# Attention scores in tiles of 64 queries of two heads, and the first row list ahead of the expert weights

## The chip, the cores and the metric

One core of one Trainium2 chip runs the whole program in one launch. The metric is the device time in microseconds (us); times before were taken in three runs, and one more execution was profiled.

## The reference

Three layers follow each other, all in float32 at the interface. Sliding-window attention with a linear distance penalty (4 batches, 8 heads, 576 positions of width 64):

```
scores = q @ k^T / 8 - slope[h] * |i - j|      where 0 <= i - j < 128, else -1e9
attn   = exp(scores - max) / (sum(exp) + 1e-9);   x = attn @ v      # 2304 rows x 512
```

Then a mixture of 8 experts: each row goes to the expert with the largest gate logit and gets `gate * (relu(x @ w1[e]) @ w2[e])`, w1 512x1024 and w2 1024x512. Then a bilinear layer: `((x @ w1) * (x @ w2) @ w3) @ w_out`, with its weights in float64.

## The kernel before

TensorE works on pairs of float32r numbers: every operand is split into a high and a low part, and a product is three matmuls, high by high, high by low, low by high (`mm3`, L278 to 281). A split is one ScalarE write (high) and one VectorE subtraction (low); in the first eight full chunks (`PE_LO = 9`) the low part of q and k is taken by a further matmul with a scaled identity instead (`split_pe`, L272 to 276, the matmul at L273), and ScalarE writes both parts.

**Attention.** A batch has four chunks of 128 queries and a tail of 64. A unit is half a chunk: two pairs of heads. There are 40 units: 24 full ones (chunks 1 to 3), 8 of chunk 0, whose window is 128 keys, and 8 tails. For a full unit, `scores` (L364) has 12 matmuls, each of one head: 64 rows of the array, 128 queries, 256 keys; head 0 of a pair lies in partitions 0 to 63 and head 1 in 64 to 127, and each writes its own PSUM tile S. A tail has both heads in one matmul of 128 rows: 64 queries of each side by side in the columns, with zeros between (`qz`), and 192 keys (`mm3`, so its lines are L279 to 281). `softmax` adds the bias and takes the smallest value in one VectorE instruction (L390), and ScalarE takes exp and the row sum (L395). `p_transposes` turns P on TensorE (L416) into one-bank PSUM tiles, tag P, two buffers: a full unit has eight transposes in two tiles, and two copies by ScalarE (L417). `attend` multiplies by v (L452). `gate_logits` transposes the result back beside the gate weights (L484), VectorE scales by 1/sum (L490), and the rows go to DRAM (`xz`). Row sums get 1e-9 and a reciprocal on VectorE (L462, L463); a tail's P is scaled before its transposes (L401 to 404).

**Beside it** run the folding of the bilinear layer's w3 and w_out into one matrix (transposes L721, products `pw`), conversions from float64 on VectorE (L676 to 689) and routing: `route` ranks a group of tiles, and GpSimd scatters row numbers into the list `inv2` (L556). What of the w3 products is left over comes behind attention.

**Hand-over.** `block_table` computes the first expert and row. `first_loads` lets the load queue (SyncE, SP in the profile) issue three weight loads of 512 KB (`load_w`, L932) and then the list of rows (`gather_x`: ids, L947), with which GpSimd gathers x (L953). The block's transposes (L974, `btp`) and splits follow, and the first expert matmuls write `ph`.

**Order.** The program is traced by a framework whose planner simulates the engines with a cost model and orders each engine's instructions by that; the engines then work in that order. Work beside the units has its places in lists by unit (`W_STEPS`, `LEAD`, `WO_AT`), which the change leaves alone.

Of the kernel before, what the change touches and what calls it, by code (L numbers as in the profile page):

```python
# [44 lines left out]
def kernel(  # L45
# [56 lines left out]
    a_p = astk.enter_context(tc.tile_pool(name="ap", bufs=2))  # L102

    def pst(tag, shape, name, bufs=2):
        return ps.tile(shape, F32, tag=tag, name=name, bufs=bufs)
# [10 lines left out]
    one_r = a_p.tile([P, H], F32, tag="one_r", name="one_r", bufs=1)  # L116
# [30 lines left out]
    bias = a_p.tile([P, H, 2 * P], F32, tag="bias", name="bias", bufs=1)  # L147
    bias_t = a_p.tile([P, H // 2, P + TAIL], F32, tag="bias_t", name="bias_t", bufs=1)
    qz = [
        [a_p.tile([P, H // 2, P], F32R, tag=f"qz{i}{j}", name=f"qz{i}{j}", bufs=1) for j in range(2)]  # L150
        for i in range(2)
    ]

# [16 lines left out]
    def build_constants():  # L170
        scr = a_p.tile([P, 3, 2 * P], F32, tag="p", name="scr", bufs=2)
        rel_i, rel, msk = scr[:, 0, :].bitcast(I32), scr[:, 1, :], scr[:, 2, :]
# [4 lines left out]
        )  # L177
        for t, f in ((id_k, -1.0), (id_q, 1.0 / SCALE)):
            nc.vector.tensor_scalar_mul(t, ident, f)

        nc.gpsimd.iota(rel_i, pattern=[[-1, 2 * P]], base=P, channel_multiplier=1)
        nc.gpsimd.tensor_copy(rel, rel_i)
        nc.gpsimd.memset(msk, 0.0)
        for t, fill in ((rel, 0.0), (msk, MASK)):
            nc.gpsimd.affine_select(
                out=t, in_=t, pattern=[[-1, 2 * P]], compare_op=ALU.is_ge, fill=fill,
                base=P, channel_multiplier=1,
            )
            nc.gpsimd.affine_select(
                out=t, in_=t, pattern=[[1, 2 * P]], compare_op=ALU.is_ge, fill=fill,  # L190
                base=-1, channel_multiplier=-1,
            )
        for h in range(H):
            slope = 2.0 ** (-8.0 * (h + 1) / H)
            nc.vector.scalar_tensor_tensor(
                out=bias[:, h, :], in0=rel, scalar=slope, in1=msk, op0=ALU.mult, op1=ALU.add
            )
# [8 lines left out]
        for i in range(2):  # L206
            for j in range(2):
                nc.gpsimd.memset(f32(qz[i][j]), 0.0)
# [4 lines left out]
    def build_constants2():  # L213
        hv = bias.rearrange("p (a t) w -> p a t w", t=2)
        nc.sync.dma_start(out=bias_t[TAIL:, :, :], in_=hv[:TAIL, :, 1, : P + TAIL])
        nc.gpsimd.tensor_copy(bias_t[:TAIL, :, :], hv[:TAIL, :, 0, : P + TAIL])
        nc.gpsimd.memset(wgx[:, :, P:], 0.0)
        nc.gpsimd.tensor_copy(wgx[:, :, :P], ident.unsqueeze(1).to_broadcast([P, ND, P]))
        nc.gpsimd.memset(one_r, 1.0)
# [50 lines left out]
    def split_pe(hi, lo, tp, scale=1.0):  # L270

        nc.scalar.activation(out=hi, in_=tp, func=AF.Copy, scale=scale)  # L272
        nc.tensor.matmul(  # L273
            tp, lhsT=id_q if scale != 1.0 else id_k, rhs=hi, start=False, stop=True, skip_group_check=True,
        )
        nc.scalar.activation(out=lo, in_=tp, func=AF.Copy, scale=scale)
# [27 lines left out]
    def transposes_q(b, c, hps=range(NP)):  # L304
        tp = pst("A", [P, NP, P], f"qtp_{b}_{c}_{hps[0]}")
        head_transposes("q", b, c, tp, hps)
        if c < NF:
            if (b, c) not in qT:
                qT[b, c] = tuple(
                    a_p.tile([P, NP, P], F32R, tag=f"qT{x}", name=f"qT{x}_{b}_{c}") for x in "hl"  # L310
                )
            hi, lo = qT[b, c]
            sl = slice(hps[0], hps[-1] + 1)
            sp = split_pe if pe_lo(b, c) else split
            sp(hi[:, sl, :], lo[:, sl, :], tp[:, sl, :], scale=-SCALE)
        else:
            hi, lo = qT[b, c] = qz[b % 2]
            for j in range(2):
                r = slice(j * D, (j + 1) * D)
                cs = slice(j * TAIL, (j + 1) * TAIL)  # L320
                split(hi[r, :, cs], lo[r, :, cs], tp[r, :, :TAIL], scale=-SCALE)
# [19 lines left out]
    st_V = {}  # L341

    def win(c):

        if c == 0:
            return 0, P
        if c < NF:
            return (c - 1) * P, 2 * P
        return (NF - 1) * P, P + TAIL

    def scores(b, c, hq):

        k0, nk = win(c)
        kh, kl = kT[b]
        qh, ql = qT[b, c]
        ks = slice(k0, k0 + nk)
        s = [pst("S", [P, 2, 2 * P], f"S_{b}_{c}_{hq}_{j}") for j in range(2 if c < NF else 1)]
        for t in range(2):
            hp = 2 * hq + t
            if c < NF:  # L360
                for i, (l, r) in enumerate(((qh, kh), (qh, kl), (ql, kh))):
                    for j in range(2):
                        d = slice(j * D, (j + 1) * D)
                        last["s"] = nc.tensor.matmul(  # L364
                            s[j][:, t, :nk], lhsT=l[d, hp, :], rhs=r[d, hp, ks],
                            start=(i == 0), stop=(i == 2),
                        )
            else:
                last["s"] = mm3(s[0][:, t, :nk], qh[:, hp, :], ql[:, hp, :], kh[:, hp, ks], kl[:, hp, ks], True, True)
        st_S[b, c, hq] = s  # L370

    def softmax(b, c, hq):
        k0, nk = win(c)
        s = st_S.pop((b, c, hq))
        if hq == 0:
            sums[b, c] = a_p.tile([P, H], F32, tag="sums", name=f"sums_{b}_{c}")
        sm = sums[b, c]
        p = a_p.tile([P, 2, 2, 2 * P], F32, tag="p", name=f"p_{b}_{c}_{hq}", bufs=2)
        mn = a_p.tile([P, 4], F32, tag="mn", name=f"mn_{b}_{c}_{hq}")
        for t in range(2):  # L380
            hp = 2 * hq + t
            for j in range(2 if c < NF else 1):
                if c == 0:
                    bi = bias[:, 2 * hp + j, P:]
                elif c < NF:
                    bi = bias[:, 2 * hp + j, :]
                else:
                    bi = bias_t[:, hp, :]
                m1 = mn[:, 2 * t + j : 2 * t + j + 1]
                nc.vector.tensor_tensor_reduce(  # L390
                    out=p[:, j, t, :nk], in0=s[j][:, t, :nk], in1=bi, scale=1.0, scalar=BIG,
                    op0=ALU.add, op1=ALU.min, accum_out=m1,
                )
                col = 2 * hp + j if c < NF else hp
                nc.scalar.activation(  # L395
                    out=p[:, j, t, :nk], in_=p[:, j, t, :nk], func=AF.Exp, scale=-1.0,
                    bias=m1, accum_out=sm[:, col : col + 1],
                )
        if c == NF:
            r1 = a_p.tile([P, 2], F32, tag="r1", name=f"r1_{b}_{hq}")  # L400
            nc.vector.tensor_scalar_add(r1, sm[:, 2 * hq : 2 * hq + 2], 1e-9)  # L401
            nc.vector.reciprocal(r1, r1)
            for t in range(2):
                nc.vector.tensor_scalar_mul(p[:, 0, t, :nk], p[:, 0, t, :nk], r1[:, t : t + 1])
        st_P[b, c, hq] = p

    def p_transposes(b, c, hq):
        p = st_P.pop((b, c, hq))
        pT = a_p.tile([P, 2, 2, 2, P], F32, tag="pT", name=f"pT_{b}_{c}_{hq}")
        if c < NF:  # L410
            nkb = 1 if c == 0 else 2
            for j in range(2):
                pt = pst("P", [P, 2, 2, P], f"PT_{b}_{c}_{hq}_{j}")
                for t in range(2):
                    for kb in range(nkb):
                        nc.tensor.transpose(pt[:, t, kb, :], p[:, j, t, kb * P : (kb + 1) * P], ident)  # L416
                nc.scalar.copy(pT[:, j, :, :nkb, :], pt[:, :, :nkb, :])  # L417
        else:
            pt = pst("P", [P, 2, 2, P], f"PT_{b}_{c}_{hq}")
            for t in range(2):  # L420
                nc.tensor.transpose(pt[:, t, 0, :], p[:, 0, t, :P], ident)
                nc.tensor.transpose(pt[:TAIL, t, 1, :], p[:, 0, t, P : P + TAIL], ident)
            nc.scalar.copy(pT[:, 0, :, 0, :], pt[:, :, 0, :])
            nc.vector.tensor_copy(pT[:TAIL, 0, :, 1, :], pt[:TAIL, :, 1, :])
        st_T[b, c, hq] = pT

    def attend(b, c, hq):
# [11 lines left out]
        if c < NF:  # L439
            kbs = [(0, c)] if c == 0 else [(0, c - 1), (1, c)]  # L440
        else:
            kbs = [(0, NF - 1), (1, NF)]
        for t in range(2):
            hp = 2 * hq + t
            for i_k, (kb, cc) in enumerate(kbs):
                n_k = P if cc < NF else TAIL
                for j in range(2):
                    if c < NF:
                        rhs = pT[:, j, t, kb, :]
                    else:  # L450
                        rhs = pT[:n_k, 0, t, kb, j * TAIL : (j + 1) * TAIL]
# [6 lines left out]
        if hq == NQ - 1:  # L458
            st_V.pop((b, c))
            if c < NF:  # L460
                r = a_p.tile([P, H], F32, tag="r", name=f"r_{b}_{c}", bufs=3)
                nc.vector.tensor_scalar_add(r, sums[b, c], 1e-9)  # L462
                nc.vector.reciprocal(r, r)  # L463
                r_t[i] = r
            else:
                r_t[i] = one_r
# [429 lines left out]
    astk.close()  # L896

# [45 lines left out]
    def gather_x(b):  # L943
# [3 lines left out]
        nc.sync.dma_start(  # L947
# [558 lines left out]
```

## Time and profile before

| | us |
|---|---|
| median of 3 runs (lowest to highest) | 776.46 (775.78 to 778.09) |
| profiled execution, its own time | 777.34 |
| its span, first to last instruction | 775.6 |
| busy: TensorE, VectorE, ScalarE, GpSimd | 750.5, 527.1, 349.5, 76.9 |

PE is TensorE's matmuls and PEld its weight loads; DVE is VectorE, ACT ScalarE, POOL GpSimd, SP the queue that issues most loads. Matmuls are pipelined: a row's length holds the fill of the array, so what one costs the engine is read from the starts. Attention takes until about 230 us of the span, the expert blocks begin at 266.60, and the bilinear layer follows to the end.

### The profile page before, as it was taken

Reading aid. Unit: us, or ns where it says so; the run is one execution under the profiler, and the core shown is the slowest. Engines: PE = TensorE matmul, PEld = TensorE weight load, DVE = VectorE, ACT = ScalarE, POOL = GpSimd, SP = SyncE. Lnnn points to the kernel's source line nnn. Section 1 sums busy time; section 2 is a strip of 40 time slices with the busy share of each in tenths; the row PEclk is TensorE's granted clock in tenths of the full one; section 3 lists DMA queues with packets and bytes.
Section 4 is the critical chain, followed back from the end, with each engine's and each line's share of the span. In section 5 each row is a group of like instructions: output and inputs, shape, how many; then the busy total and the mean of one; then the engine's idle time right before and its main releaser. Section 6 shows DMA issues by size and latency. Waiting matters only on the chain. (4 is left out here: it accounts for less than half of the span.)

```text
span 775.6 us, 12357 instructions
## 1 busy us (share of the span) xinstructions
PE 750.5 (97%) x4335; PEld 638.1 (82%) x4335; DVE 527.1 (68%) x1345; ACT 349.5 (45%) x778; POOL 76.9 (10%) x104
## 2 busy tenths in 40 slices
PE   7899999999998899999999999999999999999996
PEld 5777787777776688888888878999789997899974
DVE  3688896768589459697894345688656776567721
ACT  4786775766752333433343435432543225423131
POOL 5000200200111402021020000000120001200011
PEclk9999997899999999999999999999999999999999
DMA  7998465265127747969696335643116432234011
GB/s 139 327 304 224 110 177 144 68 147 154 42 65 142 240 123 229 292 198 341 189 302 189 120 103 180 207 136 123 63 45 200 127 111 75 65 109 120 1 42 41
DMA packets 126437, 116.62 MB, mean 150 GB/s; under 512 B 69612, under 2 KB 100716, under 8 KB 126365
## 3 DMA queue, kind: packets, MB, share of 16 engines
q1 hardware_dynamic: 122749, 106.07, 47.5%
q0 software_dynamic: 3616, 9.66, 3.9%
q8 instruction: 36, 0.59, 0.3%
q14 instruction: 36, 0.29, 0.1%
HBM read 87.85 MB, written 27.68 MB: 149 GB/s over the span
## 5 line engine op out<-in xcount | busy, mean ns | idle before, releaser
L262 ACT ACTIVATE wth<-wt 128x896 fp32r<-128x896 f32 x48 | 43.0, 945 | 90.2 <-PE pP L1252 90.2
L264 DVE TENSOR_TENSOR fwl<-fw,fwh 128x1024 fp32r<-128x1024 f32 x40 | 48.7, 1224 | 51.4 <-ACT fwh L262 51.0
L262 ACT ACTIVATE fwh<-fw 128x1024 fp32r<-128x1024 f32 x40 | 42.1, 1062 | 82.6 <-PE ph L280 65.0
L395 ACT ACTIVATE p<-p,mn 128x256 f32<-128x256 f32 (+2 forms) x144 | 68.1, 475 | 22.2 <-DVE mn L390 21.9
L279 PE MATMUL ph<-xbh,fwh 128*128 128x480 f32 x160 | 62.1, 390 | 1.1 <-ACT xbh L262 0.7
L280 PE MATMUL ph<-xbl,fwh 128*128 128x480 f32 x160 | 61.5, 384 | 0.0
L280 PE MATMUL py<-Whl,fwh 128*128 128x480 f32 x160 | 61.2, 382 | 0.0
L281 PE MATMUL ph<-xbh,fwl 128*128 128x480 f32 x160 | 61.2, 382 | 0.0
L281 PE MATMUL py<-Whl,fwl 128*128 128x480 f32 x160 | 58.9, 379 | 0.0
L279 PE MATMUL po<-Whl,abh 128*128 128x512 f32 x144 | 57.2, 397 | 0.6 <-ACT abh L262 0.6
L279 PE MATMUL py<-Whl,fwh 128*128 128x480 f32 x160 | 57.8, 379 | 0.0
L281 PE MATMUL po<-Whl,abl 128*128 128x512 f32 x144 | 57.2, 398 | 0.0
L280 PE MATMUL po<-Whl,abh 128*128 128x512 f32 x144 | 57.0, 395 | 0.0
L390 DVE CUSTOM_DVE_ANT_0 p<-S,bias 128x256 f32<-128x256 f32 (+1 forms) x128 | 43.8, 384 | 15.0 <-PE S L364 12.7
L264 DVE TENSOR_TENSOR wtl<-wt,wth 128x896 fp32r<-128x896 f32 x48 | 51.8, 1083 | 2.8 <-ACT wth L262 2.8
L264 DVE TENSOR_TENSOR abl<-ab,abh 128x512 fp32r<-128x512 f32 x36 | 24.7, 691 | 41.0 <-ACT abh L262 40.9
L1261 DVE TENSOR_TENSOR c<-pA,u 128x384 f32<-128x384 f32 x48 | 26.8, 558 | 34.6 <-PE pA L1252 32.4
L452 PE MATMUL av<-pT,vr 128*64 128x128 f32 (+2 forms) x576 | 48.7, 278 | 0.0
L262 ACT ACTIVATE abh<-ab 128x512 fp32r<-128x512 f32 x36 | 22.5, 630 | 58.1 <-PE po L280 40.6
L1357 POOL DMA_INDIRECT out_dram<-o,sid x18 | 21.6, 1202 | 259.5 <-ACT o L1356 259.5
L452 PEld LDWEIGHTS av<-pT,vr 128*64 128x64 f32 (+1 forms) x576 | 32.9, 138 | 11.7 <-issue 5.3
L416 PE MATMUL PT<-ident,p 128*128 128x128 f32 x224 | 41.5, 293 | 0.3
(249 smaller groups left out, 1959.3 us busy)
## 6 DMA issues: line engine op xcount, KB each, us to landing
wt<-wT SPq DMA_DIRECT2D x48, 448.0 KB
fw<-in_moe_w_dram SPq DMA_DIRECT2D x40, 512.0 KB
raw_w<-in_moe_w_dram SPq DMA_DIRECT2D x16, 512.0 KB
raw_m<-in_moe_w_dram SPq DMA_DIRECT2D x32, 256.0 KB
wT<-ms SPq DMA_DIRECT2D x16, 448.0 KB
yT<-zf SPq DMA_DIRECT2D x20, 256.0 KB
yT<-y SPq DMA_DIRECT2D x20, 240.0 KB
x<-yT SPq DMA_DIRECT2D x12, 384.0 KB
```

Source lines behind the costliest of these rows:

```text
L262: last["a"] = nc.scalar.activation(out=hi, in_=src, func=AF.Copy, scale=scale)
L264: last["v"] = nc.vector.tensor_tensor(out=lo, in0=src, in1=f32(hi), op=ALU.subtract)
L279: nc.tensor.matmul(dst, lhsT=lh, rhs=rh, start=start, stop=False)
L280: nc.tensor.matmul(dst, lhsT=lh, rhs=rl, start=False, stop=False)
L281: return nc.tensor.matmul(dst, lhsT=ll, rhs=rh, start=False, stop=stop)
L390: nc.vector.tensor_tensor_reduce(out=p[:, j, t, :nk], in0=s[j][:, t, :nk], in1=bi, scale=1.0, scalar=BIG, op0=ALU.add, op1=ALU.min, accum_ ...
L395: nc.scalar.activation(out=p[:, j, t, :nk], in_=p[:, j, t, :nk], func=AF.Exp, scale=-1.0, bias=m1, accum_out=sm[:, col : col + 1],)
L416: nc.tensor.transpose(pt[:, t, kb, :], p[:, j, t, kb * P : (kb + 1) * P], ident)
L452: nc.tensor.matmul(av[j * D : (j + 1) * D, hp, cs], lhsT=raw["v", b, cc][:n_k, 2 * hp + j, :], rhs=rhs, start=(i_k == 0), stop=(i_k == len ...
L1261: last["d"] = nc.vector.tensor_tensor(out=out, in0=in0, in1=in1, op=op)
L1357: sc = nc.gpsimd.indirect_dma_start(out=out, out_offset=bass.IndirectOffsetOnAxis(ap=sid[g][:, j, 0:1], axis=0), in_=o, in_offset=None, bo ...
```

## The change

All units take the tail's form. A full chunk's queries become two halves s of 64; a score tile holds 64 queries of both heads of a pair (`lhsT` is `qh[:, hp, s, :]`, 128 rows, block pattern with zeros) and 192 keys, from 64 s on within the window; S is [128, 2, 192]. Chunk 0 leaves out the keys before the start (64 and 128 remain). q's parts are written by two instructions each, one for each head's partitions, straight into the zeroed pattern `qz`, and where the low part is taken by a matmul there are two of them.

P of two halves is 384 columns, so three tiles of 128 are transposed for each pair, six in a unit. The middle tile holds the last keys of half 0 and the first of half 1; its halves are copied to their places in `pTz`, whose remaining blocks are zeroed once. The PSUM tile for it has two banks and one buffer, in a pool of its own (`psp`); tag P of the later stages comes from `ps2`. The tails' P is no longer scaled; their sums go to `sums_t` and into r as the others do. Masks are built with VectorE for 192 columns, `bias_t` and its load go, and 1e-9 is added by four GpSimd instructions.

`first_loads` reads the list of rows ahead of the three weight loads.

```
     def scores(b, c, hq):
...
+        S_t = [pst("S", [P, 2, W], f"S_{b}_{c}_{hq}_{s}") for s in halves_of(c)]
         for t in range(2):
             hp = 2 * hq + t
-            if c < NF:
-                for i, (l, r) in enumerate(((qh, kh), (qh, kl), (ql, kh))):
-                    for j in range(2):
-                        d = slice(j * D, (j + 1) * D)
-                        last["s"] = nc.tensor.matmul(
-                            s[j][:, t, :nk], lhsT=l[d, hp, :], rhs=r[d, hp, ks],
-                            start=(i == 0), stop=(i == 2),
-                        )
...
+            for s in halves_of(c):
+                w0 = first_key(c, s)
+                k0 = (c - 1) * P + s * HQ
+                ks = slice(k0 + w0, k0 + W)
+                last["s"] = mm3(
+                    S_t[s][:, t, w0:], qh[:, hp, s, :], ql[:, hp, s, :], kh[:, hp, ks], kl[:, hp, ks],
+                    True, True,
+                )
...
     def transposes_q
+        if not pe_lo(b, c):
+            for r, src, h, l in parts:
+                split(h, l, src, scale=-SCALE)
+            return
+        for r, src, h, l in parts:
+            nc.scalar.activation(out=h, in_=src, func=AF.Copy, scale=-SCALE)
+        for j in range(2):
+            nc.tensor.matmul(
+                tp[:, sl, :].rearrange("p h (s q) -> p (h s) q", s=2), lhsT=id_q,
+                rhs=hi[:, sl, :, j * HQ : (j + 1) * HQ].rearrange("p h s q -> p (h s) q"),
+                start=False, stop=j == 1, skip_group_check=True,
+            )
+        for r, src, h, l in parts:
+            nc.scalar.activation(out=l, in_=src, func=AF.Copy, scale=-SCALE)
...
     def p_transposes
+        pt = psp.tile([P, 2, 4, P], F32, tag="PT", name=f"PT_{b}_{c}_{hq}")
+        pT = pTz[n_pT[0] % 2]
...
+        tiles = [0, 2] if 0 < c < NF else [2] if c == 0 else [0]
+        for t in range(2):
+            for x in tiles:
+                tp(t, x)
+        for t in range(2):
+            tp(t, 1, P if 0 < c < NF else HQ)
+        if 0 < c < NF:
+            nc.scalar.copy(pT[:, :, 0:4:3, :], pt[:, :, 0:3:2, :])
+            nc.scalar.copy(pT[HQ:, :, 1, :], pt[HQ:, :, 1, :])
+        else:
+            x = tiles[0]
+            nc.scalar.copy(pT[:, :, 3 * x // 2, :], pt[:, :, x, :])
         if c < NF:
+            nc.scalar.copy(pT[:HQ, :, 2, :], pt[:HQ, :, 1, :])
         else:
+            nc.vector.tensor_copy(pT[:HQ, :, 2, :], pt[:HQ, :, 1, :])
...
     def attend
+                        rhs = pT[:, t, 2 * kb : 2 * kb + 2, js]
...
+                for h in range(2):
+                    for j in range(2):
+                        nc.gpsimd.tensor_scalar_add(
+                            r[h * HQ : (h + 1) * HQ, :, j], sm[j * HQ : (j + 1) * HQ, h, :], 1e-9
+                        )
...
     def build_constants
+        nc.vector.tensor_scalar_add(rel[HQ:], rel[HQ:], -float(HQ))
+        nc.vector.tensor_scalar(out=msk, in0=rel, scalar1=0.0, scalar2=None, op0=ALU.is_ge)
+        nc.vector.scalar_tensor_tensor(
+            out=seen, in0=rel, scalar=float(P), in1=msk, op0=ALU.is_lt, op1=ALU.mult
+        )
+        nc.vector.tensor_tensor(out=rel, in0=rel, in1=seen, op=ALU.mult)
+        nc.vector.tensor_scalar(
+            out=msk, in0=seen, scalar1=-MASK, scalar2=MASK, op0=ALU.mult, op1=ALU.add
+        )
...
     def first_loads(b0, b1):
-        for g in range(b0 * NS, min(b0 * NS + LA, b1 * NS)):
-            load_w(g)
+
         gather_x(b0)
+        with tc.issue_after(last["ids"].ins):
+            for g in range(b0 * NS, min(b0 * NS + LA, b1 * NS)):
+                load_w(g)
```

## Rows read from the trace of the kernel before

**Rows 1.** Busy us (instructions) by stretch; then granted clock, DMA share, GB/s.

```profile
20.00:100.00 80.00, 77.93 (x604) 59.32 (x605) 63.79 (x246) 60.84 (x188) 4.18 (x4) 0.98 0.86 243
100.00:225.00 125.00, 123.13 (x1006) 98.13 (x1005) 93.55 (x396) 83.55 (x272) 9.12 (x9) 0.95 0.44 113
```

**Rows 2.** Timeline of TensorE, scores: start us, length us, instruction, count.

```profile
17.49 0.58 PE L364 MATMUL S<-kTh,qTh 64*128 64x256 f32 x1
...
203.10 0.38 PE L364 MATMUL S<-kTh,qTh 64*128 64x256 f32 x1
...
203.80 0.28 PE L364 MATMUL S<-kTh,qTl 64*128 64x256 f32 x1
204.01 0.44 PE L416 MATMUL PT<-ident,p 128*128 128x128 f32 x2
```

**Rows 3.** Timeline of TensorE, the same for a later unit.

```profile
208.23 0.39 PE L364 MATMUL S<-kTh,qTh 64*128 64x256 f32 x2
...
208.93 0.28 PE L364 MATMUL S<-kTh,qTl 64*128 64x256 f32 x2
209.14 1.09 PE L416 MATMUL PT<-ident,p 128*128 128x128 f32 x8
```

**Rows 4.** Timeline of TensorE, scores of a tail.

```profile
217.56 0.28 PE L280 MATMUL S<-kTl,qz 128*128 128x192 f32 x1
217.68 0.27 PE L279 MATMUL S<-kTh,qz 128*128 128x192 f32 x1
217.79 0.27 PE L280 MATMUL S<-kTl,qz 128*128 128x192 f32 x1
```

**Rows 5.** Lines by shape, 0 to 260 us: count, busy us, mean ns, idle before.

```profile
L395 ACT ACTIVATE p<-p,mn 128x256 f32<-128x256 f32 x96 | 48.3, 505 | 15.6 <-DVE mn L390 15.4
L416 PE MATMUL PT<-ident,p 128*128 128x128 f32 x224 | 41.5, 293 | 0.3
L417 ACT COPY pT<-PT 128x512 f32<-128x512 f32 x48 | 27.7, 584 | 10.6 <-PE PT L416 10.2
L395 ACT ACTIVATE p<-p,mn 128x192 f32<-128x192 f32 x16 | 7.2, 452 | 4.2 <-DVE mn L390 4.2
L272 ACT ACTIVATE qTh<-qtp 128x512 fp32r<-128x512 f32 x7 | 4.1, 590 | 0.5 <-PE qtp L296 0.5
L273 PE MATMUL qtp<-qTh,id_q 128*128 128x512 f32 x7 | 3.8, 536 | 0.2
L262 ACT ACTIVATE qz<-qtp 64x256 fp32r<-64x256 f32 x8 | 3.0, 373 | 0.1
L262 ACT ACTIVATE kTh<-ktp 128x256 fp32r<-128x256 f32 x4 | 1.5, 370 | 1.2 <-PE ktp L296 1.2
```

**Rows 6.** Timeline of all engines at the start.

```profile
9.60 2.79 DVE L195 SCALAR_TENSOR_TENSOR bias<-scr 128x256 f32<-128x256 f32 x8 [6.25 <-POOL scr L189]
...
12.31 0.28 DVE L390 CUSTOM_DVE_ANT_0 p<-S,bias 128x128 f32<-128x128 f32 x1
```

**Rows 7.** Timeline of the load queue at the hand-over.

```profile
241.74 1.30 SPq L932 DMA_DIRECT2D fw<-in_moe_w_dram  x3
249.81 0.41 SPq L947 DMA_DIRECT2D ids<-inv  x1
```

**Rows 8.** Waits of the load queue, 236 to 270 us: total, times, longest.

```profile
SPq L947 <- DMA inv<-tg,pos_i: 5.4, 1, 5.4
```

**Rows 9.** Timeline of TensorE at the hand-over; in brackets the idle time before.

```profile
255.21 0.39 PE L281 MATMUL pw<-woh,w3l 128*128 128x512 f32 x1
255.44 0.60 PE L721 MATMUL w3tp<-ident,x_w 128*128 128x128 f32 x4
257.37 0.60 PE L974 MATMUL btp<-ident,xb 120*128 120x120 f32 x4 [1.33 <-issue]
...
265.31 0.63 PE L974 MATMUL btp<-ident,xb 120*128 120x120 f32 x4 [1.02 <-DVE xbl L264]
266.60 0.99 PE L279 MATMUL ph<-xbh,fwh 128*128 128x480 f32 x2 [0.66 <-ACT xbh L262]
```

More of the change, by code (lines that the diff above doesn't have):

```diff
@@ L102 @@
     a_p = astk.enter_context(tc.tile_pool(name="ap", bufs=2))
+    psp = astk.enter_context(tc.tile_pool(name="psp", bufs=1, space=PSUM))
     def pst(tag, shape, name, bufs=2):
-        return ps.tile(shape, F32, tag=tag, name=name, bufs=bufs)
+        return (ps2 if tag == "P" else ps).tile(shape, F32, tag=tag, name=name, bufs=bufs)
     ident = const.tile([P, P], F32, tag="ident", name="ident")
@@ L145 @@
     wT = dram.tile([NMC, 2, P, 7, P], F32, tag="wT", name="wT")
-    bias = a_p.tile([P, H, 2 * P], F32, tag="bias", name="bias", bufs=1)
-    bias_t = a_p.tile([P, H // 2, P + TAIL], F32, tag="bias_t", name="bias_t", bufs=1)
+    HQ = P // 2
+    W = P + HQ
+    assert TAIL == HQ and D == HQ
+    bias = a_p.tile([P, H // 2, W], F32, tag="bias", name="bias", bufs=1)
     qz = [
-        [a_p.tile([P, H // 2, P], F32R, tag=f"qz{i}{j}", name=f"qz{i}{j}", bufs=1) for j in range(2)]
+        [a_p.tile([P, H // 2, 2, P], F32R, tag=f"qz{i}{x}", name=f"qz{i}{x}", bufs=1) for x in "hl"]
         for i in range(2)
     ]
+    pTz = [a_p.tile([P, 2, 4, P], F32, tag=f"pT{i}", name=f"pT{i}", bufs=1) for i in range(2)]
     raw = {}
@@ L306, in transposes_q @@
         head_transposes("q", b, c, tp, hps)
-        if c < NF:
[L308 to L321, printed above, removed]
+        n_h = 2 if c < NF else 1
+        hi, lo = qT[b, c] = qz[(b * (NF + 1) + c) % 2]
+        sl = slice(hps[0], hps[-1] + 1)
+        parts = []
+        for j in range(2):
+            r = slice(j * D, (j + 1) * D)
+            if n_h == 2:
+                src = tp[r, sl, :].rearrange("p h (s q) -> p (h s) q", s=2)
+                dst = [t[r, sl, :, r].rearrange("p h s q -> p (h s) q") for t in (hi, lo)]
+            else:
+                src = tp[r, sl, :HQ]
+                dst = [t[r, sl, 0, r] for t in (hi, lo)]
+            parts.append((r, src, *dst))
+        if not pe_lo(b, c):
[12 more added lines that the diff above has]
+            nc.scalar.activation(out=l, in_=src, func=AF.Copy, scale=-SCALE)
     def transposes_k(b, c, hps=range(NP)):
@@ L379, in softmax @@
+        st_S[b, c, hq] = S_t
+    def softmax(b, c, hq):
+        S_t = st_S.pop((b, c, hq))
+        i = tidx[b, c]
+        if i not in sums:
+            tag, bufs = ("sums", 2) if c < NF else ("sums_t", 1)
+            sums[i] = a_p.tile([P, 2, NP], F32, tag=tag, name=f"{tag}_{i}", bufs=bufs)
+        sm = sums[i]
+        p = a_p.tile([P, 2, 2, W], F32, tag="p", name=f"p_{b}_{c}_{hq}", bufs=2)
         mn = a_p.tile([P, 4], F32, tag="mn", name=f"mn_{b}_{c}_{hq}")
@@ L381, in softmax @@
             hp = 2 * hq + t
[L382 to L389, printed above, removed]
+            for s in halves_of(c):
+                w0 = first_key(c, s)
+                m1 = mn[:, 2 * t + s : 2 * t + s + 1]
                 nc.vector.tensor_tensor_reduce(
-                    out=p[:, j, t, :nk], in0=s[j][:, t, :nk], in1=bi, scale=1.0, scalar=BIG,
-                    op0=ALU.add, op1=ALU.min, accum_out=m1,
+                    out=p[:, t, s, w0:], in0=S_t[s][:, t, w0:], in1=bias[:, hp, w0:], scale=1.0,
+                    scalar=BIG, op0=ALU.add, op1=ALU.min, accum_out=m1,
@@ L393, in softmax @@
                 )
-                col = 2 * hp + j if c < NF else hp
+                col = s if c < NF else b % 2
                 nc.scalar.activation(
-                    out=p[:, j, t, :nk], in_=p[:, j, t, :nk], func=AF.Exp, scale=-1.0,
-                    bias=m1, accum_out=sm[:, col : col + 1],
-                )
[L399 to L404, printed above, removed]
+                    out=p[:, t, s, w0:], in_=p[:, t, s, w0:], func=AF.Exp, scale=-1.0,
+                    bias=m1, accum_out=sm[:, col, hp : hp + 1],
+                )
@@ L405, in softmax @@
         st_P[b, c, hq] = p
     def p_transposes(b, c, hq):
-        p = st_P.pop((b, c, hq))
-        pT = a_p.tile([P, 2, 2, 2, P], F32, tag="pT", name=f"pT_{b}_{c}_{hq}")
-        if c < NF:
[L411 to L417, printed above, removed]
-        else:
[L419 to L424, printed above, removed]
+        p = st_P.pop((b, c, hq)).rearrange("p t s w -> p t (s w)")
@@ L459, in attend @@
             st_V.pop((b, c))
-            if c < NF:
-                r = a_p.tile([P, H], F32, tag="r", name=f"r_{b}_{c}", bufs=3)
-                nc.vector.tensor_scalar_add(r, sums[b, c], 1e-9)
+            if c < NF or b % 2 == 1:
+                sm = sums.pop(i)
+                r = a_p.tile([P, NP, 2], F32, tag="r", name=f"r_{b}_{c}", bufs=3)
+                for h in range(2):
+                    for j in range(2):
+                        nc.gpsimd.tensor_scalar_add(
+                            r[h * HQ : (h + 1) * HQ, :, j], sm[j * HQ : (j + 1) * HQ, h, :], 1e-9
+                        )
+                r = r.rearrange("p c j -> p (c j)")
                 nc.vector.reciprocal(r, r)
                 r_t[i] = r
-            else:
-                r_t[i] = one_r
     o_t = {}
@@ L896 @@
     astk.close()
+    ps2 = ctx.enter_context(tc.tile_pool(name="ps2", bufs=2, space=PSUM))
     f_p = ctx.enter_context(tc.tile_pool(name="fp", bufs=2))
@@ L946, in gather_x @@
         ids = x_p.tile([P, NU, 2], I32, tag="ids", name=f"ids_{b}", bufs=deep(2))
-        nc.sync.dma_start(
+        last["ids"] = nc.sync.dma_start(
             out=ids[:RU], in_=inv2[ds(row, BLK), :].rearrange("(u p) o -> p u o", p=RU)
```

74 lines of the change are left out of this document (27 added, 47 removed).

## The prediction

> **What bounds the kernel now.** I read the table by stretches first, then the list of instructions by line and shape, then single stretches of the timeline, and last the waits of the load queue. In the attention stage TensorE hardly rests: 77.93 of 80 us and 123.13 of 125 us are busy, against 63.79 and 93.55 for VectorE and 60.84 and 83.55 for ScalarE [rows 1]. A busy TensorE isn't one at its peak, so I looked at starts: in most places each matmul starts as soon as the one before lets it, about 0.11 us apart for weights of 128 columns, and the waits between are short. So the order that the planner wrote for TensorE is dense, and what a matmul costs there is its distance to the next start. The rest of the kernel (expert blocks and bilinear layer) is not touched, except for the hand-over into it, where TensorE does wait: 1.33, 1.02 and 0.66 us within ten microseconds [rows 9].
>
> **The change part by part.**
>
> *Scores.* A full unit (two pairs of heads, 128 queries, 256 keys) has 12 matmuls before and 12 after. Before, each contracts over 64 rows and two of them may run beside each other in the two halves of the array; after, each contracts over 128 rows, half of its weights zero, for 192 keys. I counted through the timeline what the units before do. In 11 of the 24, the first at 17.49 and the last at 203.10, the planner put the six matmuls of one head of each pair in a run of their own, so nothing runs beside anything: six take from 203.10 to the next instruction at 204.01, 0.91 us [rows 2], and with some 0.09 us more on the way in, two runs make 2.0 us. In the others the two heads run together: 12 take from 208.23 to 209.14, 0.91 us, again 1.0 us with the way in [rows 3]; most of these are cut into two or three runs and pay the way in and out each time (about 0.1 us each), which makes some 1.25 us. The mean is (11 x 2.0 + 13 x 1.25) / 24 = 1.59 us. After: the tails of 64 queries already have this form, 128 rows and 192 keys, and start 0.12 and 0.11 us apart [rows 4], so 12 make 1.38 us at 0.115 each. That is 0.21 us less, 5.0 us for 24 units. Bounds: 0.38 x 24 = 9 us more if all of them had been paired in one run, 15 us less if none. I take the counted mix. First chunks (8 units) go the same two ways at shorter length; I take nothing for them.
>
> The Trainium skill, "TensorEngine Tiling (Array Packing)", section "Performance Considerations", speaks against this part: with a contraction of 64 or less one is to tile the rows by two and gains up to twice. By that rule alone the change costs the 9 us of the upper bound. The same page, "Key Properties", says that changing the tiling mode drains TensorE; [rows 2, 3] show both, the pairing in one and its absence in the other, each with a slow first and last step. The count decides, and the sum stands without the page.
>
> *Transposes of P.* Six for eight in a full unit. Eight take 1.09 us with the last one's 0.29 in it [rows 3, 5], so (1.09 - 0.29) / 7 = 0.11 us apart: 2 x 0.11 x 24 = 5.3 us less. First chunks and tails keep four.
>
> *The split of q.* Its high and low parts now go into a block pattern, so each is written in two halves of 64 partitions. ScalarE's time follows the width, not the partitions: 64x256 takes 373 ns where 128x256 takes 370 [rows 5], so a half is priced as a whole, 0.59 us. In the eight chunks that take the low part by a matmul (all in the first half of the stage) ScalarE gets 2 x 0.59 x 8 = 9.4 us more, and TensorE one more matmul of 512 columns each: between 0.23 us (the distance of such a matmul to the next start, from 255.21 to 255.44 [rows 9]) and its whole 0.54 us [rows 5]; I take 0.3, so 2.4 us more. In the eight others ScalarE gets 4.7 us more and VectorE about as much.
>
> *Softmax and copies.* An exponential over 192 instead of 256 saves 505 - 452 = 53 ns, 96 times: 5.1 us less for ScalarE [rows 5]. Copies of transposed P: two of 584 ns become one of 584 and two of 64x256 at 373, 0.16 us more in each of 24 units, 3.9 us. VectorE sheds a quarter of its columns in the reduction, the scaling of the tails' P, and the sums' addition, which goes to GpSimd. I cost that addition at nothing: four small instructions ahead of a reciprocal that the tile of x waits for, with a unit of other work between. GpSimd's queue is in order, and the scatters of routed rows stand in it: an addition put behind a scatter that still waits would hold x, and the PSUM buffer it is read from, by the length of a group's scatters; between 0 and a few us in all, and I take 0.
>
> *ScalarE by halves.* From 20 to 100 us it goes from 60.84 to 60.8 + 9.4 - 2.6 + 1.9 = 69.6 of 80, 87%; from 100 to 225 from 83.55 to 83.6 + 4.7 - 2.6 + 1.9 = 87.6 of 125, 70%. So in the second half TensorE's saving, 2.5 + 2.65 = 5.1 us, should come out nearly whole: I take 5. In the first, TensorE's 2.5 + 2.65 - 2.4 = 2.75 us meet a ScalarE that has little room: I take 1, with bounds of 2.8 gained and 8.8 lost (all that ScalarE gets more).
>
> *The start.* Before, the eight bias instructions of VectorE begin at 9.60 us after 6.25 us of waiting for GpSimd's masks, and the first reduction comes at 12.31 [rows 6]. After, the masks are five short VectorE instructions. But TensorE has transposes to do in that time, and each of the first q splits is one ScalarE write longer twice. Bounds: 4 gained, 2 lost; I take 1 gained.
>
> *The hand-over.* The first list of rows (ids) is issued at 249.81, though the three weight loads before it are out 1.30 us after 241.74 [rows 7]; for 5.4 us of that the load queue waits for the scatter's landing [rows 8], whose small packets share the DMA engines with 1.5 MB of weights. Now the list goes first, so the scatter lands alone. The weights go out some 3 us later, and are split only behind the transposes at 255.44 [rows 9], 10 us on: hidden. With the rows there early, the transposes at 257.37 and 265.31 need no wait, and their splits are done before the last weight products end: 1.33 + 1.02 + 0.66 = 3.0 us [rows 9], and at most 0.3 more that TensorE's re-entry costs. I take 3.3; bounds 0 (the planner leaves them where they are) and 5.
>
> **Sum.** 5 + 1 + 1 + 3.3 = 10.3 us less than the profiled run's 777.34 us (775.6 span and 1.7 around it): 767.0. That run lies 0.9 us over the median of 776.46, so about 766.
>
> **Rivals.**
> 1. *ScalarE becomes the bound of the first half.* For it: 87% of an engine that works in order, and whose copies and exponentials TensorE waits for. Against: until 100 us its waits were for others. Price: the 1 us gained there turns into about 6 lost, so 776.5 - 10.3 + 7 = 773.
> 2. *Slower: the single buffer of transposed P.* P's transposes had two PSUM buffers of half a unit each; now one of two banks serves a whole unit, so the next unit's first transpose waits for three copies in a row, 0.58 + 0.37 + 0.37 = 1.33 us, behind whatever exponentials ScalarE has queued. If TensorE's order has nothing else there, 0.9 us stand open in each of 24 units: 22 us, giving 766 + 22 = 788. It turns slower than before from about 0.45 us a unit. Against it: av products, scores and weight products of about 3 us lie between two units' transposes, and the planner knows the buffer.
> 3. *More than forecast: the clock.* From 100 to 225 us the granted clock is 0.95 on average [rows 1]; of its two levels, 1.2 and 2.4 GHz, the lower one then held for about 12 us of the 125, and dense work loses 6 us by it. With fewer waits some of that may come back, and the first half's saving may come whole: 766 - 8 = 758. That it falls more often instead lies in rival 1's price.
> 4. *It doesn't pay in attention at all*: latency between engines, not TensorE, sets the pace. Then only the start and the hand-over are left, 772.
>
> **How the numbers follow.** Forecast 0.52 (761 to 771), rival 3 0.13 (754 to 760), rivals 1 and 4 0.21 (771 to 777), rival 2 0.14 (779 to 792). Within 0.3% is 774.1 to 778.8, about what can be told from no change; a third of rivals 1 and 4 lies there. So faster 0.79, same 0.07, slower 0.14. The range, 755 to 777, leaves out rival 2 and the far end of rival 3.
>
> **What would show it.** Scores of full units 0.11 us apart in runs without slow first steps; 48 transposes fewer; ScalarE near 87% from 20 to 100 us, with TensorE's idle time there no longer than now; the hand-over's first expert matmul about 3 us nearer to the last weight product. Waits of TensorE for copies of P would mean rival 2; scores that start more than 0.13 us apart, or a stage from 100 to 225 us no shorter, would make the prediction wrong.

## The result, and the profile after

The changed kernel took 778.1 us (median of 20 runs) against 775.9 for the kernel before (20 runs). The ratio is 1.0063, 95% interval [1.0037, 1.0090]: 0.6% slower. The ratio is that of the means, 779.1 to 774.2 us, without four runs of the kernel before that lie over 1.5% above its fastest; with them the means differ by 3.5 us in place of 4.9. Forecast were 766 us and a range of 755 to 777. The profiled run took 779.8 us and has a span of 778.1.

The stretches that answer to [rows 1], with the same columns:

```profile
20.00:100.00 80.00, 71.61 (x585) 59.71 (x584) 59.48 (x236) 66.85 (x204) 11.71 (x28) 0.96 0.81 236
100.00:225.00 125.00, 114.34 (x940) 95.19 (x941) 89.08 (x352) 87.00 (x288) 21.54 (x53) 0.95 0.44 114
```

TensorE (first column after the length) rests 19 us where it rested 4, and comes less far: the last instruction of the routing on it (cnt) starts at 242.20 us for 237.58. (That it starts 940 matmuls for 1,006 in the second stretch is in part the transposes left out.) ScalarE (fourth) has 84% and 70%; forecast were 87% and 70%.

TensorE's own work did get shorter. A full unit in the timeline, beside [rows 2, 3]:

```profile
208.28 0.35 PE L287 MATMUL S<-kTh,qz1h 128*128 128x192 f32 x1
208.48 0.27 PE L288 MATMUL S<-kTl,qz1h 128*128 128x192 f32 x1
...
209.59 0.27 PE L289 MATMUL S<-kTh,qz1l 128*128 128x192 f32 x1
210.26 0.87 PE L422 MATMUL PT<-ident,p 128*128 128x128 f32 x6 [0.39 <-ACT pT L437]
```

Scores start 0.11 us apart, transposes are six for eight; then comes the new thing, a wait for ScalarE's third copy of the unit before. Lines by shape up to 260 us, beside [rows 5]:

```profile
L407 ACT ACTIVATE p<-p,mn 128x192 f32<-128x192 f32 x112 | 50.0, 449 | 8.3 <-DVE mn L402 7.7 <-DVE cand L546 0.3
L422 PE MATMUL PT<-ident,p 128*128 128x128 f32 x176 | 34.0, 301 | 4.5 <-ACT p L407 2.1 <-ACT pT L437 2.0
L431 ACT COPY pT<-PT 128x512 f32<-128x512 f32 x24 | 14.0, 582 | 7.0 <-PE PT L422 4.6 <-PE qtp L304 2.2
L437 ACT COPY pT<-PT 64x256 f32<-64x256 f32 x32 | 11.7, 366 | 0.6
L341 ACT ACTIVATE qz1l<-qtp 64x512 fp32r<-64x512 f32 x8 | 4.7, 589 | 0.0
L335 PE MATMUL qtp<-qz1h,id_q 128*128 128x512 f32 x8 | 3.1, 477 | 1.3 <-ACT qz1h L333 1.3
```

The durations are those of the prediction: 449 ns for an exponential (452 taken), 582 and 366 for the copies (584 and 373), 589 for half a split of q (590). The idle time before them is what changed.

To see the whole, I summed for all attention instructions the distance to the next start, at the higher clock and without waits (worked out from the timeline, us):

```
                           before   after   e1
scores (432)                51.5    52.9   52.7
transposes of P (256, 208)  33.7    25.7   25.7
av products (576)           43.1    40.3   40.3
x and logits (144)          21.1    17.4   17.2
q transposes, low parts     12.1    13.0   13.2
sum                        161.5   149.3  149.1
changes of tiling form       285     169    172
waits of TensorE, 5-250 us  13.5    28.6   26.6
```

The scores don't show their gain in their own row: a change of form (the rows and columns of the array that an instruction uses) is paid by the last instruction ahead of it, which is an av product, a transpose or a logits product. Before, the next start comes 0.11 us behind a transpose where another transpose of the same form follows, and 0.20 us where a score over 64 rows does (medians over attention). The work is 12.2 us less; the waits are 15 us more. Where work ends and a wait begins is a choice: with the idle times that the profile itself gives for TensorE, the work is 10.0 us less (9.0 in e1) and the waits are 14.4 us more (12.6 in e1).

The start answers to [rows 6], the hand-over to [rows 7 to 9] (VectorE; the load queue and its wait; TensorE):

```profile
5.90 3.43 DVE L205 SCALAR_TENSOR_TENSOR bias<-scr 64x192 f32<-64x192 f32 x8
9.36 0.23 DVE L402 CUSTOM_DVE_ANT_0 p<-S,bias 128x64 f32<-128x64 f32 x1
```

```profile
249.82 0.43 SPq L969 DMA_DIRECT2D ids<-inv  x1
251.30 2.13 SPq L954 DMA_DIRECT2D fw<-in_moe_w_dram  x4
```

```profile
SPq L969 <- DMA inv<-tg,pos_i: 3.7, 1, 3.7
```

```profile
268.03 0.63 PE L996 MATMUL btp<-ident,xb 120*128 120x120 f32 x4 [0.55 <-DVE xbl L272]
268.91 0.63 PE L996 MATMUL btp<-ident,xb 120*128 120x120 f32 x4 [0.25 <-DVE xbl L272]
270.20 0.70 PE L287 MATMUL ph<-xbh,fwh 128*128 128x480 f32 x2 [0.66 <-issue]
```

The first reduction comes 2.95 us earlier, the list goes ahead of the weights and waits 1.7 us less for the scatter, and TensorE's waits of 3.0 us are 1.46. Yet the first expert matmul starts at 270.20, where it was 266.60: attention was already late.

Where it got late is plain on GpSimd's timeline (start, length, instruction; in brackets idle time before and what ended it):

```profile
151.97 0.95 POOL L577 DMA_INDIRECT inv<-tg,pos_i  x1 [0.30 <-issue]
153.00 0.51 POOL L482 TENSOR_SCALAR r<-sums 64x4 f32<-64x4 f32 x1
160.03 0.78 POOL L482 TENSOR_SCALAR r<-sums 64x4 f32<-64x4 f32 x3 [6.53 <-DMA inv<-tg,pos_i]
```

and on that of all engines right behind:

```profile
160.85 0.20 DVE L486 RECIPROCAL r<-r 128x8 f32<-128x8 f32 x1 [7.43 <-POOL r L482]
160.97 0.63 DVE L274 SCALAR_TENSOR_TENSOR qz1l<-qtp,qz1h 64x512 fp32r<-64x512 f32 x1
161.63 0.59 ACT L270 ACTIVATE qz1h<-qtp 64x512 fp32r<-64x512 f32 x1 [5.53 <-DVE qz1l L274]
...
162.28 0.53 PE L287 MATMUL S<-kTh,qz1h 128*128 128x192 f32 x1 [4.99 <-ACT qz1h L270]
```

Read it from the top: five scatters are issued, the first of four additions runs, and the second waits 6.53 us until all five have landed. VectorE has the reciprocal next in its order and stands 7.43 us; behind it waits q's split, behind that ScalarE's, and behind that TensorE, 4.99 us. In the trace the second addition behind each of three groups of scatters has such a wait; GpSimd's waits in all:

```profile
POOL r L482 <- DMA inv<-tg,pos_i: 12.6, 3, 6.5
```

Only the longest of the three stops TensorE for long. About the other two, from 84 to 100 us and from 203 to 215 us, TensorE has no wait above 0.7 us.

Then the clock. The same 20 us of this kernel and of e1_sums_on_vector (below), columns as in [rows 1]:

```profile
160.00:180.00 20.00, 17.67 (x114) 16.08 (x115) 10.49 (x46) 12.40 (x39) 1.53 (x7) 0.66 0.36 90
```

```profile
160.00:180.00 20.00, 19.16 (x173) 15.81 (x171) 15.92 (x74) 14.28 (x51) 0.00 (x0) 1.00 0.53 135
```

Behind the stall the granted clock is 0.66 on average: the lower of its two levels, 1.2 GHz, for two thirds of the stretch. 114 matmuls start in place of 173. The Trainium skill, "TensorE: Matmul & The Clock Gate", section "Part 1: The HAM clock gate", says that the array falls to the lower level after idling and that activity releases it; this place agrees, with 0.66 behind a wait of 4.99 us.

### The profile page after: what moved, and what is told of

Its sections match the earlier page's. It is cut to its first block, busy times and chain, and to the rows that moved or that the text cites. A ratio compares the mean times of both kernels' runs of the same rounds, so it can differ in the third digit from the quotient of the medians.

```text
span 778.1 us, 12375 instructions
## 1 busy us (share of the span) xinstructions
PE 740.4 (95%) x4296; PEld 641.0 (82%) x4296; DVE 524.1 (67%) x1314; ACT 363.9 (47%) x828; POOL 96.6 (12%) x171
## 5 line engine op out<-in xcount | busy, mean ns | idle before, releaser
L407 ACT ACTIVATE p<-p,mn 128x192 f32<-128x192 f32 (+2 forms) x144 | 61.7, 431 | 13.6 <-DVE mn L402 13.0
L402 DVE CUSTOM_DVE_ANT_0 p<-S,bias 128x192 f32<-128x192 f32 (+2 forms) x144 | 41.4, 329 | 20.1 <-PE S L289 18.3
L468 PE MATMUL av<-pT,vr 128*64 128x128 f32 (+2 forms) x576 | 46.9, 285 | 1.7 <-ACT pT L432 1.2
L468 PEld LDWEIGHTS av<-pT,vr 128*64 128x64 f32 (+1 forms) x576 | 32.3, 142 | 13.5 <-issue 5.7
L422 PE MATMUL PT<-ident,p 128*128 128x128 f32 x208 | 37.7, 299 | 4.5 <-ACT p L407 2.1
```

The lines of the kernel that those rows point to most:

```text
L402: nc.vector.tensor_tensor_reduce(out=p[:, t, s, w0:], in0=S_t[s][:, t, w0:], in1=bias[:, hp, w0:], scale=1.0, scalar=BIG, op0=ALU.add, op1 ...
L407: nc.scalar.activation(out=p[:, t, s, w0:], in_=p[:, t, s, w0:], func=AF.Exp, scale=-1.0, bias=m1, accum_out=sm[:, col, hp : hp + 1],)
L422: nc.tensor.transpose(pt[:n, t, x, :], p[:, t, x * P : x * P + n], ident)
L468: nc.tensor.matmul(av[j * D : (j + 1) * D, hp, cs], lhsT=raw["v", b, cc][:n_k, 2 * hp + j, :], rhs=rhs, start=(i_k == 0), stop=(i_k == len ...
```

## The experiments

Each ratio is to the kernel before, run on the same chip. An edit also changes the planner's order of TensorE's work. Read from the traces, 117 of 4,296 matmuls stand outside the common order of the changed kernel and e1, 122 for e9, 403 between e1 and e11, and 222 of 4,335 between e7 and e10. Only e2 and e3 have the order of the kernel that they derive from (in e2 a single matmul differs).

**e1: the additions on VectorE** (from the changed kernel)

```
-                        nc.gpsimd.tensor_scalar_add(
+                        nc.vector.tensor_scalar_add(
```

> The four additions of 1e-9 go from GpSimd to VectorE, all else as in the changed kernel. Theory A (GpSimd's queue): one addition behind the scatters held the next scores for 5.0 us and the low clock after it cost some 6 us more, so 5 to 10 us less than the changed kernel, 768 to 773. Theory B (ScalarE and the single buffer of transposed P make the waits of TensorE): the stall was covered by other lateness, within 2 us of the changed kernel, 776 to 780.

770.76 us, ratio 0.9937 [0.9905, 0.9968]: theory A, and faster than both kernels. It is 1.3% less than the changed kernel, whose interval it doesn't touch.

**e2: the hand-over alone** (from before), **e3: all but the hand-over** (from the changed kernel)

```
-        for g in range(b0 * NS, min(b0 * NS + LA, b1 * NS)):
-            load_w(g)
...
+        with tc.issue_after(last["ids"].ins):
+            for g in range(b0 * NS, min(b0 * NS + LA, b1 * NS)):
+                load_w(g)
```

In e2 the loads go behind the first gather of rows; e3 is the same edit backwards.

> The kernel before, with the first row list ahead of the three weight loads and nothing else. If the hand-over gains by itself what the two traces show between the last count of routed rows and the first product of w2 (36.2 for 38.5 us): 2 to 3 us less than before. Rival: the planner's order hides it, or the weights then come late: no change.

> The changed kernel with the weight loads ahead of the row list again. If the hand-over gains: 2 to 3 us more than the changed kernel, 780 to 781. If it is worth nothing: 778.

e2 took 772.69 us, 0.9966 [0.9934, 0.9998]; e3 780.86 us, 1.0071 [1.0040, 1.0103]. Alone the edit is worth 2.6 us (0.2 to 5.1), as expected for e2 and near the 3.3 forecast. That it is worth as much in the changed kernel isn't shown by the times: the intervals of 1.0071 and 1.0063 overlap. Where the gain arises is taken up below.

**e4: the third copy of P on VectorE as well** (from e1)

```
-        if c < NF:
-            nc.scalar.copy(pT[:HQ, :, 2, :], pt[:HQ, :, 1, :])
-        else:
-            nc.vector.tensor_copy(pT[:HQ, :, 2, :], pt[:HQ, :, 1, :])
+        nc.vector.tensor_copy(pT[:HQ, :, 2, :], pt[:HQ, :, 1, :])
```

> As the first of these, and one of the two half copies of transposed P goes from ScalarE to VectorE: 32 copies of 64x256 off ScalarE, 12 us less of its work, and the chain of three copies behind the single PSUM buffer one shorter. Theory B: 3 to 6 us less than the first of these. Theory A alone: the same as the first within 1 us.

772.03 us, 0.9957 [0.9925, 0.9988]: no gain over e1, so theory B's 3 to 6 us don't come. TensorE's waits stay (26.3 us).

**e5: two PSUM buffers for transposed P** (from e1)

```
+        for t in range(2):
+            pt = psp.tile([P, 4, P], F32, tag="PT", bufs=2)
+            ...  # three transposes, two copies on ScalarE, one on VectorE
```

> The additions of the sums on VectorE as in e1_sums_on_vector (770.8 us), and the transposed P of each pair of heads in a one-bank PSUM tile of its own, two buffers instead of one of two banks; the third copy of each on VectorE. Theory: in e1 TensorE waited 5.9 us up to 250 us behind ScalarE's copies out of the single buffer (rival 2 of the prediction in small); with two buffers most of it goes: 766 to 768 us, those waits under 2 us. Rival: the buffer only takes the place of another wait (exponentials, x), ScalarE's or the chain's pace rules: 769 to 773 us, and the waits come back under other names.

779.99 us, 1.0066 [1.0037, 1.0095]: a miss for both. TensorE's longest waits from 20 to 225 us (total, times, longest), first of e1, then of e5:

```profile
PE PT L422 <- ACT pT L437: 2.8, 4, 1.0
PE av L468 <- ACT pT L432: 1.6, 2, 0.9
```

```profile
PE PT L425 <- DVE pT L432: 1.6, 4, 0.5
PE xlg L498 <- ACT oT L466: 1.4, 1, 1.4
PE av L461 <- ACT oT L466: 1.4, 3, 0.5
```

Waits fall from 26.6 to 22.6 us, but with smaller tiles the planner mixes transposes and av products more: 247 changes of form for 172, and the five rows of the table add up to 158.0 us for 149.1. Rival 2 in small was there (the first of e1's two lines; in the second, av products wait for a copy's result, which another buffer wouldn't change). This remedy costs more than it saves.

**e6: q's low parts by subtraction on VectorE**, **e8: e5 and e6 together** (from e1)

```
-        if not pe_lo(b, c):
-            for r, src, h, l in parts:
-                split(h, l, src, scale=-SCALE)
-            return
-        ...  # the low parts by a matmul with the identity
+        for r, src, h, l in parts:
+            split(h, l, src, scale=-SCALE)
```

> e1_sums_on_vector (770.8 us), and the low parts of q in all chunks by VectorE's subtraction, none by a matmul with the identity: 16 matmuls and 16 copies of 64 partitions fewer on TensorE and ScalarE in the first half, 16 subtractions more on VectorE. Theory (rival 1 of the prediction: ScalarE, 98% busy from 40 to 60 us, bounds the first half): 765 to 769 us, with fewer waits of TensorE for q's parts (4.4 us in e1 by the low parts of q and k together). Rival: VectorE's additional work delays the reductions as much: 770 to 774 us.

> The edits of e5_two_buffers_for_pt and e6_q_low_parts_on_vector together on e1_sums_on_vector (770.8 us). Theory: both waits were separate, their gains add: 762 to 766 us. Rival: they are the same slack seen from two sides, or VectorE becomes the bound: 766 to 772 us.

e6: 774.07 us, 0.9995 [0.9963, 1.0026]; e8: 781.61 us, 1.0075 [1.0042, 1.0109]. Both theories fall. e6 ends at the upper edge of its rival's range (770 to 774), and e8 lies above its rival's (766 to 772) too. In e6 q's row of the table drops from 13.2 to 8.5 us, and the waits rise from 26.6 to 31.1; VectorE is busy for 74.2 of the 80 us from 20 to 100, 65.8 in e1.

**e7: the failed step alone** (from before), **e10: the same in one piece** (from before), **e9: the changed kernel with one piece**

```
e7   -  nc.vector.tensor_scalar_add(r, sums[b, c], 1e-9)
     +  for h in (slice(0, 64), slice(64, 128)):
     +      for j in range(2):
     +          nc.gpsimd.tensor_scalar_add(rr[h, :, j], sm[h, :, j], 1e-9)
e10  +  nc.gpsimd.tensor_scalar_add(r, sums[b, c], 1e-9)
e9   +  nc.gpsimd.tensor_scalar_add(sm, sm, 1e-9)
     +  ...  # reciprocals in four pieces on VectorE
```

> The kernel before (775.8 us) with one edit: the addition of 1e-9 to the sums goes from VectorE to GpSimd in four pieces of 64 partitions, as in the changed kernel. Theory: this step alone, which the prediction costed at nothing, loses time: the second piece behind each of three groups of scatters waits for their landing (up to 6.5 us in the changed kernel), TensorE stalls by 2 to 5 us there and the granted clock falls behind it: 778 to 782 us. Rival: the stall needs the rest of the change (its lower dense work, or ScalarE's longer splits of q in the same chain); alone the piece has slack: 775 to 777 us.

> The kernel before with the addition on GpSimd in one piece (one word of the code changed); no addition waits for a landing. e7_sums_on_gpsimd_alone, the same in four pieces, of which the second behind each of three groups of scatters waits for the landing, took 795.4 us. Theory: the landing makes the difference: 775 to 780 us. Rival: the four pieces' place in the queue and the new order of TensorE's work that the planner makes of it cost as much without a landing: 788 to 797 us.

> The changed kernel with the addition left on GpSimd, but in one piece, in place on the sums, and the four pieces made by VectorE's reciprocals instead. In the built order no addition waits any more for the landing of scatters, though additions still stand behind scatters in GpSimd's queue. Theory: what cost time in the changed kernel (778.1 us) is the wait for the landing, not GpSimd as such: 769 to 773 us, near e1_sums_on_vector (770.8), without a stall of 5 us on TensorE. Rival: the way over GpSimd itself (one engine more in the chain from the last exponential to x, an instruction behind the issue of four scatters) costs it: 775 to 779 us.

e7: 795.39 us, 1.0266 [1.0223, 1.0308], a loss far beyond the 778 to 782 us expected. e10: 777.91 us, 1.0050 [1.0016, 1.0085], in its theory's range. e9: 773.09 us, 0.9967 [0.9934, 1.0000], at the upper edge of its theory's. In e9 and e10 no addition waits for a landing. Four pieces or one: 2.2% apart on the kernel before, 1.0% on the changed one, on the same engine with the same arithmetic. Who waited for the addition, in e7 and in e10 (us, times):

```profile
  DVE r L467: 15.7, 8
```

```profile
  DVE r L463: 5.8, 8
```

e7's third group of scatters shows the chain again, GpSimd first, then VectorE, then TensorE, then the clock behind it:

```profile
206.08 0.96 POOL L560 DMA_INDIRECT inv<-tg,pos_i  x1 [0.30 <-issue]
207.11 0.22 POOL L466 TENSOR_SCALAR r<-sums 64x4 f32<-64x4 f32 x1
212.87 0.78 POOL L466 TENSOR_SCALAR r<-sums 64x4 f32<-64x4 f32 x3 [5.54 <-DMA inv<-tg,pos_i]
```

```profile
213.68 0.20 DVE L467 RECIPROCAL r<-r 128x8 f32<-128x8 f32 x1 [5.07 <-POOL r L466]
213.80 0.37 DVE L390 CUSTOM_DVE_ANT_0 p<-S,bias 128x256 f32<-128x256 f32 x1
```

```profile
214.58 0.58 PE L364 MATMUL S<-kTh,qTh 64*128 64x256 f32 x1 [3.45 <-DVE mn L390]
```

```profile
212.00:232.00 20.00, 17.42 (x136) 14.11 (x136) 10.51 (x49) 13.71 (x45) 1.96 (x9) 0.74 0.11 34
```

Here no split of q stands behind the reciprocal but a unit's reductions; the scores need the PSUM tile that these read.

**e11: less work on VectorE**, **e12: less on ScalarE** (from e1)

```
e11  -  ...  # five instructions that rebuild a piece of w3 or w_out
     +  nc.vector.tensor_scalar_mul(x, high.bitcast(F32), 1.0)
e12  -  nc.scalar.copy(pT[HQ:, :, 1, :], pt[HQ:, :, 1, :])
     -  nc.scalar.copy(pT[:HQ, :, 2, :], pt[:HQ, :, 1, :])
     ...  # and VectorE's copy for the tails; the blocks stay zero
```

> e1_sums_on_vector (770.8 us), and the rebuilding of the fp64 weights w3 and w_out left out: one VectorE instruction of 512 columns for each of 23 pieces in place of five (by the lines of the changed kernel 0.41 + 0.68 + 0.43 + 0.69 us less apiece, some 50 us of VectorE up to 250 us). The weights are wrong by that, the work of the other engines is the same. Question: whose latency holds TensorE's waits of attention, 26.6 us in e1 by my count. Theory: the chain from the scores over VectorE's reduction and ScalarE's exponential to the transposes waits behind such VectorE work: attention ends 4 to 8 us earlier, 763 to 767 us. Rival: ScalarE's queue holds it: 769 to 772 us.

> e1_sums_on_vector (770.8 us), and the two copies of 64x256 of each unit's transposed P left out (their place stays zero, so the output and perhaps the routing change; 0.37 us each, 20.5 us of ScalarE and the last third of each unit's PSUM buffer time). Theory: ScalarE's queue and the single buffer hold attention back: it ends 4 to 8 us earlier than in e1, 763 to 767 us where the routing asks for as many blocks. Rival: VectorE's chain or the planner's order holds it: 769 to 772 us, waits come back under other names.

e11: 764.94 us, 0.9853 [0.9814, 0.9891], in the theory's range. e12's routing asks for more blocks (1,159.5 us), so only its attention can be read. The stretches of e11, then of e12:

```profile
20.00:100.00 80.00, 72.35 (x624) 60.62 (x622) 45.11 (x230) 71.35 (x216) 4.04 (x4) 1.00 0.92 261
100.00:225.00 125.00, 119.69 (x1026) 99.97 (x1024) 84.54 (x413) 87.64 (x294) 11.67 (x12) 1.00 0.47 108
```

```profile
20.00:100.00 80.00, 72.09 (x621) 60.91 (x621) 64.84 (x265) 63.53 (x194) 4.22 (x4) 1.00 0.85 248
100.00:225.00 125.00, 119.71 (x1023) 99.48 (x1023) 101.53 (x446) 77.16 (x256) 12.21 (x12) 1.00 0.48 115
```

To compare attention in all runs I take the start of the routing's last instruction on TensorE (cnt), with time at the lower clock counted half, and split it into TensorE's idle times, as the profile gives them, and the rest (worked out from the timelines, us). The record of the clock begins at 13 to 26 us of each span. What lies before is counted as the lower level, since matmuls there start at about twice the distance: in the kernel before, scores that run alone start 0.21 us apart there and 0.12 later.

```
                                  cnt     rest    idle
before                           216.8   210.5     6.3
e2, same order                   219.1   210.6     8.5
e10, one piece on GpSimd         220.0   213.4     6.6
e7, four pieces                  228.7   211.7    16.9
changed kernel                   221.5   199.9    21.6
e3, same order                   220.0   199.0    21.0
e9, one piece on GpSimd          221.9   203.6    18.2
e1, on VectorE                   218.1   201.4    16.7
e11, less VectorE                213.5   199.7    13.8
e12, less ScalarE                215.8   201.1    14.7
```

The two pairs of the same order tell how far this start varies from one execution to another: 2.3 and 1.5 us. e11's start is 4.6 us earlier than e1's, twice that, and its time is 0.84% (6.5 us) shorter, with intervals that don't touch: relief of VectorE shortens attention. e12's 2.3 us are no more than the variation, and less than the 4 to 8 expected; that relief of ScalarE shortens attention isn't shown.

## Why the prediction was wrong

Forecast were 10.3 us less, measured is 0.63% of 776 us, 4.9 us more: 15.2 us apart.

- **The step that failed: "I cost that addition at nothing"** ("between 0 and a few us in all, and I take 0"). The text named the mechanism, an addition behind a scatter, and bounded it by "a few us". From the changed kernel to e1 it measures 1.0063 - 0.9937 = 1.26%, 9.8 us (the means of the runs lie 8.7 apart). Of these 7.4 (by the means 6.6, to e9) go with the pieces that wait for the landing; the 2.3 left for the way over GpSimd are within the intervals of e1 and e9. Alone, the step costs the kernel before 20.6 us in four pieces and 3.9 in one. I read what an addition would queue behind, not that one which hasn't itself to wait can be given the wait for a landing, nor that VectorE has other work behind the reciprocal.
- **How it costs.** Over all timed runs the mean granted clock is 0.983 in the changed kernel, 0.990 in e1, 0.993 in e9; 0.979 in e7, 0.991 in e10. An estimate of the time lost to the lower level, (1 - clock) times the span, is 13.4, 7.8, 5.1, 16.5 and 7.3 us; 9.3 for the kernel before. (The first 13 to 26 us, ahead of the clock's record, are not in it.) At full clock, span times clock, the changed kernel is 0.8 us shorter than before (763.6 for 764.4), too little to be told from none, and e9 2.2 longer than it. So in the changed kernel the loss shows mostly in the clock. In e7, 7.2 us more at full clock than e10 come with 9.2 of clock. The table of attention shows why the two pairs differ: e7 idles 10.3 us more than e10 with about the same rest, while the changed kernel idles 3.4 us more than e9 with a rest that is 3.7 us shorter, in another order.
- **Attention: TensorE's term was right, its worth was not.** Scores, transposes and what stands next to them fell by 161.5 - 149.3 = 12.2 us (10.0 by the profile's idle times), against 5.0 + 5.3 - 2.4 = 7.9 forecast (less for q's split, more for changes of form). But "in the second half TensorE's saving should come out nearly whole" fell. With the addition repaired the waits grow from 13.5 to 26.6 us, up to cnt from 6.3 to 16.7, and take it back: cnt starts at 218.1 us in e1, and at 216.8 and 219.1 in the two runs with the order before. e1's 770.8 us lie inside the forecast's range, but not by attention's saving; how its 4.9 us (2.5 to 7.4) divide into hand-over, start and clock isn't shown. Rival 4 (772: the latency between engines sets the pace) describes e1, and e11 shows that VectorE's part of the chain is one that holds TensorE.
- **Rival 1** had ScalarE's load right (84% for 87%; its sum makes 69.5 us, not 69.6), but e4 and e6 took work from ScalarE and gained nothing. Both gave it to VectorE, and e12, which doesn't, gains nothing clear of the variation. **Rival 2**, the single buffer, was there with 2.8 of e1's waits from 20 to 225 us, an eighth of the 22 priced. **Rival 3** had its sign wrong for the changed kernel (0.983 for 0.988); e1's 0.990 isn't clear of noise.
- **Start and hand-over.** The first reduction is 2.95 us earlier for the 1 forecast in all; what that is worth at the end isn't shown. The hand-over was mis-sized: e3 and the changed kernel have one order, and from cnt to the first product of w2 they take 37.40 and 36.17 us with 3.02 and 1.76 us of waits, 1.2 us for the 3.3 forecast. In e2 this stretch takes 37.02 us for 38.52 before, of which 3.4 us lie at the lower clock in the kernel before and none in e2; without that the two are equal, and the waits are 4.12 us for 4.43. So e2's gain in time isn't seen at its hand-over. The 0.3 us for TensorE's re-entry rested on no row, and no run shows it. In e1 the same stretch has a new wait of 2.97 us ahead of the block's transposes and takes 37.79 us.

Open: why the built program gives the second addition the waits for the landing. And how much of e1's new waits an order made for the new lengths would save.

## What to carry to other kernels

An instruction moved to an engine that issues indirect DMAs is priced by the waits it gets in the built program, and by what stands behind its reader; "off the critical path" holds for GpSimd's time, not for VectorE's reciprocal. When TensorE's waits are short, shorter matmuls may buy waits first: here ten microseconds less of TensorE's work left attention as long as it was, and less of VectorE's shortened it. One profile of a kernel says little about two microseconds: compare runs of the same order first. A change of tiling form is paid by the instruction ahead of it, so look for its gain in the neighbours' rows.

## What the runs showed of the hardware

A scatter of five pieces was issued in 6.2 us (146.69 to 152.92), and the addition that waits for all five started 7.1 us later. A change of form on TensorE cost 0.09 us: behind a transpose the next start came after 0.11 us without one and 0.20 with one (medians before). A stall of 4.99 us on TensorE in the changed kernel and one of 3.45 us in e7 were followed by a granted clock of 0.66 and 0.74 over 20 us. In e3, which has the changed kernel's order and the same stall (4.96 us, until 164.92), it is 0.83 from 163 to 183 us, so what a stall costs varies. And the lower level also comes without such a stall: before, from 100 to 140 us, it is 0.84 while TensorE rests 1.4 us, so a long stall isn't its only occasion:

```profile
100.00:140.00 40.00, 38.63 (x277) 31.10 (x277) 31.27 (x118) 22.80 (x77) 0.00 (x0) 0.84 0.57 146
```
